# Strassen's seven-block product for the first matmul of the second feed-forward layer, operands in one arena

## The chip, the core and the metric

The kernel runs on one core of a Trainium2 chip. The metric is device time in microseconds (us) of one execution. Engines are named as the profile names them: PE is the matrix engine (PEld its weight loads), DVE the vector engine, ACT the scalar engine, POOL the GpSimd engine, SP the engine that issues the DMAs. "Columns" are the elements per partition that an instruction streams: a matmul of 384 columns has a 128 x 384 moving operand against a 128 x 128 stationary one.

## What is computed

Block-local attention over chunks of 64 makes x (2304 tokens x 512). Two feed-forward layers follow:

```python
def _moe_ref(x, w_in, w_out):                  # layer 1, 2048 features
    h = np.maximum(x @ w_in, 0.0)
    return (h * h @ w_out).astype(np.float32)

def _moe2_ref(x, domain_probs, w1, w2):        # layer 2, E = 4 experts of F = 1024 features
    p = domain_probs / (domain_probs.sum(-1, keepdims=True) + 1e-09)
    out = np.zeros((N, D), dtype=np.float32)
    for e in range(E):
        h = np.maximum(x @ w1[e], 0.0)
        out += p[:, e:e + 1] * (h @ w2[e])
    return out
```

The sizes are N = 2304 tokens, D = 512, E = 4, F = 1024. All inputs of layer 2 are float32. The change concerns `x @ w1[e]`.

## The kernel before

**Split operands.** Every float32 operand of a product is kept as two halves in the type float32r, hi (a rounded copy, written by ACT) and lo (what the copy leaves out, by a subtraction). Each product is three matmuls: hi by hi, hi by lo, lo by hi.

**Steps.** Both layers run in passes of G = 4 feature tiles of 128. Layer 1 has 4 passes, layer 2 has 8 (two for each expert). A pass goes over five token blocks of 384, 384, 512, 512 and 512 tokens (`BLOCKS`), and over the 4 feature tiles in each: 20 steps a pass, 80 steps for layer 1 and 160 for layer 2. A step of `l1` (matmul line L286) multiplies 4 slices of the inner dimension by 3 products, 12 matmuls as wide as the block, into one PSUM bank. ACT and DVE make the hidden tile's halves `gh` and `gl` from it (in layer 2 lines L305 and L307; in layer 1 there is a square between, L297 to L301). A step later `l2` (L332) multiplies them into accumulators. In layer 1 these are 4 x 3 matmuls as wide as the block. In layer 2 the hidden tile is the stationary operand and the weights move, so each 128 tokens take 3 matmuls of 512 columns: 9 a step in a block of 384, 12 in one of 512.

**Evacuation.** After 4 feature tiles the accumulators leave PSUM: in layer 1 by L365 and L367, in layer 2 by L378 (first pass) and L380 (the others: multiply by the expert's probability and add). The last pass's tiles go out by DMA (L385).

**Between the layers.** `split_x` (L347 on ACT, L348 on DVE) makes the halves of layer 1's result while layer 1 still runs.

**Weights.** SP loads a unit of 256 KB (L107), ACT copies it (L145), POOL subtracts (L146). In layer 2 each weight is loaded once. Four units of hidden weights and four of output weights are held in each of two rings.

**Order.** `tc.manual_schedule()` keeps the instructions in the order of the text on each engine, and each engine works its queue in that order. The framework adds the waits that the operands need. PSUM has eight banks: one with the tag "h", four "a", three "t".

Of the kernel before, what the change touches and what calls it, by code (L numbers as in the profile page):

```python
# [42 lines left out]
def tile_kernel(ctx, tc, q, k, v, moe_w_in, moe_w_out, moe2_p, moe2_w1, moe2_w2, out):  # L43
# [13 lines left out]
    npass = npass1 + E * nf2 // G  # L57
# [3 lines left out]

    const = ctx.enter_context(tc.tile_pool(name="const", bufs=1))
    xp = ctx.enter_context(tc.tile_pool(name="xp", bufs=1))
    wpa = ctx.enter_context(tc.tile_pool(name="wpa", bufs=RING_A))
    rawp = ctx.enter_context(tc.tile_pool(name="rawp", bufs=RAW_BUFS))
    cvp = ctx.enter_context(tc.tile_pool(name="cvp", bufs=CV_BUFS))
    gp = ctx.enter_context(tc.tile_pool(name="gp", bufs=LAG + 1))
    rp = ctx.enter_context(tc.tile_pool(name="rp", bufs=1))
    ps = ctx.enter_context(tc.tile_pool(name="ps", bufs=1, space=bass.MemoryType.PSUM))
    att = ExitStack()  # L70
    qkp = att.enter_context(tc.tile_pool(name="qkp", bufs=2))
    late = {}

# [10 lines left out]
    raw, cv, halves = {}, {}, {}  # L84

    def unit_load(n, which):
        if n < nf1:
            r = rawp.tile([P, DM, 2], I32, tag="raw", name="raw")
            if which == 0:
                nc.sync.dma_start(  # L90
                    out=r.rearrange("p (k f) w -> p k (f w)", k=KD),
                    in_=moe_w_in[:, 2 * n * P:2 * (n + 1) * P].rearrange("(k p) f -> p k f", p=P),
                )
            else:
                nc.sync.dma_start(
                    out=r.rearrange("p f w -> p (f w)"), in_=moe_w_out[n * P:(n + 1) * P, :]
                )
        else:
            e, f = divmod(n - nf1, nf2)
            r = rawp.tile([P, DM], F32, tag="raw", name="raw")  # L100
            if which == 0:
                nc.sync.dma_start(
                    out=r.rearrange("p (k f) -> p k f", k=KD),
                    in_=moe2_w1[e, :, f * P:(f + 1) * P].rearrange("(k p) f -> p k f", p=P),
                )
            else:
                nc.sync.dma_start(out=r, in_=moe2_w2[e, f * P:(f + 1) * P, :])  # L107
        raw[n, which] = r

    def unit_convert(n, which):  # L110
        """float64 (two 32-bit words) to the nearest float32; beyond float32's range it
        saturates, below its normal range it becomes zero."""
        r = raw.pop((n, which))
        if n >= nf1:
            cv[n, which] = r
            yield
            return
# [22 lines left out]
    def unit_split(n, which):  # L140
        a = cv.pop((n, which))
        pool = wpa if n % (RING_A + RING_B) < RING_A else late["w"]
        h = pool.tile([P, DM], F32R, tag=f"h{which}", name=f"h{which}")
        l = pool.tile([P, DM], F32R, tag=f"l{which}", name=f"l{which}")
# [7 lines left out]
    # Heads j and j+4 (x = 0, 1) share a tile of 128 partitions.  # L152
# [8 lines left out]
    def new_x(tb):  # L161
        xh[tb] = xp.tile([P, KD, BLOCKS[tb]], F32R, tag=f"xh{tb}", name=f"xh{tb}")
        xl[tb] = xp.tile([P, KD, BLOCKS[tb]], F32R, tag=f"xl{tb}", name=f"xl{tb}")
# [111 lines left out]
    steps = [(p, tb, f) for p in range(npass) for tb in range(NB) for f in range(G)]  # L275
# [3 lines left out]
    def l1(i):  # L279
# [12 lines left out]
        hi = gp.tile([P, 512], F32R, tag="gh", name="gh")  # L292
        lo = gp.tile([P, 512], F32R, tag="gl", name="gl")
        gh[i], gl[i] = hi, lo
        if p < npass1:
            r = rp.tile([P, 512], F32, tag="r", name="r")
            nc.scalar.activation(out=r[:, :T], in_=ph[:, :T], func=AF.Relu)  # L297
            nc.vector.tensor_tensor(out=r[:, :T], in0=r[:, :T], in1=r[:, :T], op=ALU.mult)  # L298
            yield
            nc.scalar.copy(hi[:, :T], r[:, :T])  # L300
            nc.vector.tensor_tensor(  # L301
                out=lo[:, :T], in0=r[:, :T], in1=hi[:, :T].bitcast(F32), op=ALU.subtract
            )
        else:
            nc.scalar.activation(out=hi[:, :T], in_=ph[:, :T], func=AF.Relu)  # L305
            yield
            nc.vector.scalar_tensor_tensor(  # L307
                out=lo[:, :T],
                in0=ph[:, :T],
                scalar=0.0,  # L310
                in1=hi[:, :T].bitcast(F32),
                op0=ALU.max,
                op1=ALU.subtract,
            )

    def l2(i):
# [4 lines left out]
        for d in range(KD if p < npass1 else T // P):  # L321
# [3 lines left out]
            if p < npass1:  # L325
                o = pacc[d][:, :T]
                prods = ((bh[:, ds], hi[:, :T]), (bh[:, ds], lo[:, :T]), (bl[:, ds], hi[:, :T]))
            else:
                o = pacc[d]
                prods = ((hi[:, ds], bh), (hi[:, ds], bl), (lo[:, ds], bh))  # L330
# [8 lines left out]
    later = []  # L339

    def split_x(n):
        for _ in range(min(n, len(later))):
            tb, d = later.pop(0)
            if d == 0:
                new_x(tb)
            a = acc[tb][:, d, :]
            nc.scalar.copy(xh[tb][:, d, :], a)  # L347
            nc.vector.tensor_tensor(  # L348
                out=xl[tb][:, d, :], in0=a, in1=xh[tb][:, d, :].bitcast(F32), op=ALU.subtract
            )  # L350

    def new_acc(tb, shape):
        pool = xp if tb < ACC_EARLY else late["x"]
        acc[tb] = pool.tile(shape, F32, tag=f"acc{tb}", name=f"acc{tb}")

    def evacuate(p, tb, d):
        T = BLOCKS[tb]
        nt = T // P
        pa = pacc.pop(d)
        if p < npass1:  # L360
            if p == 0 and d == 0:
                new_acc(tb, [P, KD, T])
            a = acc[tb][:, d, :]
            if p == 0:
                nc.scalar.copy(a, pa[:, :T])  # L365
            else:
                nc.vector.tensor_tensor(out=a, in0=pa[:, :T], in1=a, op=ALU.add)  # L367
            if p == npass1 - 1:
                later.append((tb, d))
        else:  # L370
            if p == npass1 and d == 0:
                new_acc(tb, [P, nt, DM])
# [48 lines left out]
    with tc.manual_schedule():  # L421
# [44 lines left out]
        for which in range(2):  # L466
            s0_stage(0, "ttthaaaa", which)
# [70 lines left out]
```

## Time and profile before

| | |
|---|---|
| time, median of 3 runs | 1301.8 us (1301.67 to 1302.4) |
| span of the profiled execution, first to last instruction | 1300.4 us |
| PE busy | 1265.9 us, 97% |
| PEld busy | 1088.6 us, 84% |
| DVE busy | 517.0 us, 40% |
| ACT busy | 329.8 us, 25% |
| POOL busy | 209.9 us, 16% |
| mean granted PE clock | 0.986 |

The span lies 1.4 us under the median. The times of single instructions, and the place of each, are those of the one profiled execution. A matmul's end is modelled, and successive matmuls overlap in the record, so the pace of PE is read from the distance between the starts of matmuls and not from the duration of one. The page cuts the span into 40 slices of 32.5 us: attention and layer 1 fill the first 15 of them or so, layer 2 the rest.

### The profile page before, as it was taken

The page shows a single profiled execution, that of the slowest core. Times are in us where ns is not written, and L with a number is a line of the kernel's source. Part 1 is how long each engine was busy: PE and PEld are TensorE (multiplying, and loading weights), DVE is VectorE, ACT ScalarE, POOL GpSimd, SP SyncE. Part 2 cuts the span into 40 slices and gives each one's busy share as a digit, 9 for nine tenths or more (in the row PEclk, how much of TensorE's full clock was granted, in tenths as well). Part 3 has the DMA queues.
Part 4 walks back from the last instruction along what each step waited for, and adds up shares of the span by engine and source line. Part 5 has one row for each costly group of instructions (what it writes and reads, how often), then busy time and mean ns, then how long its engine had stood idle before and what let it go on. Part 6 is the DMA issues. An engine that isn't in the chain of part 4 may idle for free.

```text
span 1300.4 us, 16632 instructions
## 1 busy us (share of the span) xinstructions
PE 1265.9 (97%) x6952; PEld 1088.6 (84%) x6952; DVE 517.0 (40%) x902; ACT 329.8 (25%) x615; POOL 209.9 (16%) x166
## 2 busy tenths in 40 slices
PE   5799997999999999999999999999999999999998
PEld 4698886989989988888888888888888888888887
DVE  5976768664763554111222222222222222222222
ACT  3555543332332333322111111111111111111110
POOL 2420145431440110100110110110110110110000
PEclk7799998999999999999999999999999999999999
DMA  7846022210100000000000100100100100100011
GB/s 191 181 102 160 18 67 66 61 52 18 49 27 14 25 25 17 25 25 14 28 25 9 33 25 9 33 25 9 33 25 9 33 25 9 33 1 1 34 49 65
DMA packets 94843, 53.55 MB, mean 41 GB/s; under 512 B 61744, under 2 KB 86320, under 8 KB 94768
## 3 DMA queue, kind: packets, MB, share of 16 engines
q1 hardware_dynamic: 94768, 52.48, 14.6%
q8 instruction: 55, 0.90, 0.3%
q14 instruction: 20, 0.16, 0.0%
HBM read 47.75 MB, written 4.72 MB: 40 GB/s over the span
## 4 chain that ended last, share of the span: by engine, by line
PE 92%; DVE 5%; issue 1%; SPq 1%; ACT 1%; DMA 0%
PE psa L332 45%; PE pst L286 31%; PE psh L286 13%; PE pst L257 1%; PE pst L215 1%; PE pst L200 1%; DVE cv L122 1%; DVE cv L123 1%; DVE cv L132 1%; PE pst L242 1%; DVE r L298 0%; DMA raw<-in_moe_w_in 0%; SPq L188 0%; SPq L179 0%; DVE e L222 0%
## 5 line engine op out<-in xcount | busy, mean ns | idle before, releaser
L286 PE MATMUL pst<-xh,l 128*128 128x512 f32 (+1 forms) x672 | 247.8, 369 | 0.0
L286 PE MATMUL pst<-xh,h 128*128 128x512 f32 (+1 forms) x672 | 247.5, 368 | 0.0
L286 PE MATMUL pst<-xl,h 128*128 128x512 f32 (+1 forms) x672 | 247.4, 368 | 0.0
L332 PE MATMUL psa<-h,gl 128*128 128x512 f32 x576 | 225.4, 391 | 0.0
L332 PE MATMUL psa<-l,gh 128*128 128x512 f32 x576 | 225.2, 391 | 0.0
L332 PE MATMUL psa<-h,gh 128*128 128x512 f32 x576 | 224.0, 389 | 0.0
L146 POOL TENSOR_TENSOR l<-raw,h 128x512 fp32r<-128x512 f32 x64 | 82.6, 1291 | 705.2 <-ACT h L145 705.2
L305 ACT ACTIVATE gh<-pst 128x512 fp32r<-128x512 f32 (+1 forms) x120 | 66.7, 556 | 496.6 <-PE pst L286 496.6
L307 DVE SCALAR_TENSOR_TENSOR gl<-pst,gh 128x512 fp32r<-128x512 f32 (+1 forms) x120 | 76.1, 634 | 278.2 <-ACT gh L305 278.2
L380 DVE SCALAR_TENSOR_TENSOR acc<-psa,prob,acc 128x512 f32<-128x512 f32 x126 | 89.1, 744 | 151.9 <-PE psa L332 151.9
L286 PEld LDWEIGHTS pst<-xl,h 128*128 128x128 f32 x672 | 126.1, 188 | 18.2
L286 PEld LDWEIGHTS pst<-xh,h 128*128 128x128 f32 x672 | 126.2, 188 | 18.1
L286 PEld LDWEIGHTS pst<-xh,l 128*128 128x128 f32 x672 | 126.1, 188 | 15.9
L332 PE MATMUL psa<-gh,h 128*128 128x512 f32 (+1 forms) x320 | 121.3, 379 | 6.7 <-ACT gh L300 6.0
L332 PEld LDWEIGHTS psa<-h,gl 128*128 128x128 f32 x576 | 108.1, 188 | 22.7
L332 PEld LDWEIGHTS psa<-l,gh 128*128 128x128 f32 x576 | 108.1, 188 | 21.2
L332 PEld LDWEIGHTS psa<-h,gh 128*128 128x128 f32 x576 | 108.1, 188 | 20.7
L332 PE MATMUL psa<-gl,h 128*128 128x512 f32 (+1 forms) x320 | 118.8, 371 | 0.7 <-DVE gl L301 0.7
L332 PE MATMUL psa<-gh,l 128*128 128x512 f32 (+1 forms) x320 | 118.4, 370 | 0.0
L286 PE MATMUL psh<-xl,h 128*128 128x384 f32 (+1 forms) x288 | 106.7, 370 | 3.4 <-DVE xl L270 3.4
L286 PE MATMUL psh<-xh,h 128*128 128x384 f32 (+1 forms) x288 | 109.0, 378 | 0.0
L286 PE MATMUL psh<-xh,l 128*128 128x384 f32 (+1 forms) x288 | 106.6, 370 | 0.0
(92 smaller groups left out, 1282.3 us busy)
## 6 DMA issues: line engine op xcount, KB each, us to landing
raw<-in_moe_w SPq DMA_DIRECT2D x64, 256.0 KB, 2.8
raw<-in_moe_w_in SPq DMA_DIRECT2D x16, 512.0 KB, 4.0
raw<-in_moe_w_out SPq DMA_DIRECT2D x16, 512.0 KB, 3.7
out<-acc SPq DMA_DIRECT2D x18, 256.0 KB, 2.0
q<-in_q SPq DMA_DIRECT2D x32, 128.0 KB, 3.5
k<-in_k SPq DMA_DIRECT2D x32, 128.0 KB, 3.2
v<-in_v SPq DMA_DIRECT2D x32, 80.0 KB, 3.0
v<-in_v SPq DMA_DIRECT2D x32, 64.0 KB, 2.7
```

The costliest lines, as they stand in the source:

```text
L122: nc.vector.tensor_scalar(out=a, in0=hi, scalar1=0x7FFFFFFF, scalar2=None, op0=ALU.bitwise_and)
L123: nc.vector.tensor_scalar(out=af, in0=af, scalar1=F64_MIN, scalar2=F64_MAX, op0=ALU.max, op1=ALU.min)
L132: nc.vector.scalar_tensor_tensor(out=a, in0=a, scalar=0x7FFFFFFF, in1=hi, op0=ALU.bitwise_and, op1=ALU.bitwise_or)
L146: nc.gpsimd.tensor_tensor(out=l, in0=a, in1=h.bitcast(F32), op=ALU.subtract)
L200: nc.tensor.transpose(out=pt[:, j, :], in_=a[:, j].rearrange("p x d -> p (x d)"), identity=ident)
L215: nc.tensor.matmul(pt[x][cs, j, :], lhsT=qt[r, j, cs], rhs=kt[r, j, cs], start=True, stop=True)
L242: nc.tensor.transpose(out=pt[:, j, :], in_=e[:, j, :], identity=ident)
L286: nc.tensor.matmul(ph[:, :T], lhsT=w[:, kk, :], rhs=x[tb][:, kk, :], start=(kk == 0 and n == 0), stop=(kk == KD - 1 and n == 2),)
L305: nc.scalar.activation(out=hi[:, :T], in_=ph[:, :T], func=AF.Relu)
L307: nc.vector.scalar_tensor_tensor(out=lo[:, :T], in0=ph[:, :T], scalar=0.0, in1=hi[:, :T].bitcast(F32), op0=ALU.max, op1=ALU.subtract,)
L332: nc.tensor.matmul(o, lhsT=w, rhs=y, start=(f == 0 and n == 0), stop=(f == G - 1 and n == 2))
L380: nc.vector.scalar_tensor_tensor(out=a, in0=pa, scalar=pe, in1=a, op0=ALU.mult, op1=ALU.add)
```

## The change

Layer 2 is written anew, and layer 1 keeps its steps.

- The 2304 tokens form three groups of 768, and each group goes through all experts before the next begins. Each step n (48 in all) takes one group and two feature tiles of one expert.
- In a step, `x @ w1` for two halves of 384 tokens, two halves of the inner dimension and two feature tiles is eight block products. Strassen's scheme (in Winograd's form) makes them of seven: `c_unit` runs seven units of 2 x 3 = 6 matmuls of 384 columns, on sums and differences of blocks, into three PSUM accumulators b, c and d. `c_finish` snapshots b three times (`snap`, ACT), adds the snapshots to c and d (DVE) and makes the four hidden tiles (`hidden`: ACT, then DVE).
- `d_unit` makes the output of 128 tokens from the two feature tiles of the step before: 6 matmuls of 512 columns into one bank. `d_finish` evacuates it after those 6 (before, after 12). The units of c and d alternate on PE.
- The sums of x (`y_combine`) and those of the weights (`w1_add`) are made by POOL. Their halves are made by ACT and POOL (weights), and ACT with DVE or POOL (x). Since the three groups go through all weights in turn, each weight is loaded, summed and split three times.
- All float32r operands lie in one SBUF tile, the arena `ar`. Layer 1's x, its first ring of weights and the hidden halves are slices of it too, and layer 2's operands reuse their places.
- `split_x` goes. The preparation of layer 2's first group (`y_combine(0)`, the first `w1_add` and `w1_split`) runs during layer 1's last pass.

The diff, cut to what the text below speaks of:

```diff
+HALF = 384
+NSUP = 3
+SWAP = 63
...
+    XW = 2 * KD * NT
+    AR = XW + RING_A * 4 * DM + (LAG + 1) * 2 * 512
+    ar = arena.tile([P, AR], F32R, name="ar")
+    RING_AT, GP_AT = XW, XW + RING_A * 4 * DM
+    NY, NW, NG = 14 * 2 * HALF, 14 * 2 * P, 8 * HALF
+    Y_AT = 0
+    W1_AT = [NY + NW + 4 * DM + NG, NY]
+    W2_AT = [W1_AT[0] + NW, NY + NW]
+    G_AT = [W2_AT[0] + 4 * DM, NY + NW + 4 * DM]
+    assert G_AT[0] + NG <= AR
...
+            o = RING_AT + (n % RING_A * 4 + 2 * which) * DM
+            h, l = ar[:, o:o + DM], ar[:, o + DM:o + 2 * DM]
+        else:
+            h = late["w"].tile([P, DM], F32R, tag=f"h{which}", name=f"h{which}")
+            l = late["w"].tile([P, DM], F32R, tag=f"l{which}", name=f"l{which}")
...
+        o, w = 2 * KD * starts[tb], KD * BLOCKS[tb]
+        xh[tb] = ar[:, o:o + w].rearrange("p (k t) -> p k t", k=KD)
+        xl[tb] = ar[:, o + w:o + 2 * w].rearrange("p (k t) -> p k t", k=KD)
...
+        o = GP_AT + i % (LAG + 1) * 1024
+        hi, lo = ar[:, o:o + 512], ar[:, o + 512:o + 1024]
...
+    def sub(o, a, b):
+        nc.gpsimd.tensor_tensor(out=o, in0=a, in1=b, op=ALU.subtract)
...
+        if sp == 0:
+            for i in (Y11, Y21, Y22):
+                yield from y_split(sp, i)
+        sub(t1, y12, y11)
+        yield
+        sub(t3, y22, y12)
+        yield
+        sub(t2, y22, t1)
+        yield
+        sub(t4, y21, t2)
...
+    def y_split(sp, i):
+        h, l = y_slot(i)
+        a = comb[sp][i]
+        nc.scalar.copy(h, a)
+        eng = nc.vector if sp == 0 or i % 2 == 0 else nc.gpsimd
+        eng.tensor_tensor(out=l, in0=a, in1=h.bitcast(F32), op=ALU.subtract)
...
+    def w1_add(n, part):
+        r = raw1[n]
+        o, a, b, op = (
+            (4, 0, 3, ALU.add), (5, 4, 1, ALU.subtract), (6, 1, 0, ALU.subtract), (7, 2, 5, ALU.subtract)
+        )[part]
+        nc.gpsimd.tensor_tensor(out=r[:, o], in0=r[:, a], in1=r[:, b], op=op)
...
+    def w1_split(n, part):
+        c = NW // 4
+        if part == 0:
+            o = W1_AT[n % 2]
+            w1c[n] = ar[:, o:o + NW // 2], ar[:, o + NW // 2:o + NW]
+        h, l = (y[:, part * c:(part + 1) * c] for y in w1c[n])
+        a = raw1[n].rearrange("p s k f -> p (s k f)")[:, 2 * P + part * c:2 * P + (part + 1) * c]
+        nc.scalar.copy(h, a)
+        nc.gpsimd.tensor_tensor(out=l, in0=a, in1=h.bitcast(F32), op=ALU.subtract)
...
+    UNITS = ((0, Y11), (1, Y21), (4, T2), (3, T1), (5, T3), (2, T4), (6, Y22))
+    g, st = {}, {}
+    def c_unit(n, u):
+        ws, ys = UNITS[u]
+        if u == 0:
+            st["b"] = bank("t")
+            o = G_AT[n % 2]
+            g[n] = [
+                [ar[:, o + (2 * i + z) * HALF:o + (2 * i + z + 1) * HALF] for z in range(2)] for i in range(4)
+            ]
+        elif u == 1:
+            st["c"] = bank("h")
+        elif u == 3:
+            st["d"] = bank("t")
+        p = st["bcbdbbd"[u]][:, :HALF]
...
+        for kk in range(2):
+            for z, (w, y) in enumerate(((wh, yh), (wh, yl), (wl, yh))):
+                nc.tensor.matmul(
+                    p, lhsT=w[:, kk, :], rhs=y[:, kk, :],
+                    start=(kk == 0 and z == 0 and u in (0, 1, 3)),
+                    stop=(kk == 1 and z == 2 and u in (1, 5, 6)),
+                    skip_group_check=True,
...
+    def snap(nm, p):
+        s = st[nm] = late["s"].tile([P, HALF], F32, tag=nm, name=nm)
+        nc.scalar.copy(s, p)
+    def hidden(n, i, p):
+        h, l = g[n][i]
+        nc.scalar.activation(out=h, in_=p, func=AF.Relu)
+        nc.vector.scalar_tensor_tensor(
+            out=l, in0=p, scalar=0.0, in1=h.bitcast(F32), op0=ALU.max, op1=ALU.subtract
+        )
+    def c_finish(n, u):
+        b, c, d = (st[x][:, :HALF] if x in st else None for x in "bcd")
+        if u == 0:
+            snap("s1", b)
+        elif u == 1:
+            nc.vector.tensor_tensor(out=c, in0=c, in1=st["s1"], op=ALU.add)
+            hidden(n, 0, c)
+        elif u == 2:
+            snap("u2", b)
+        elif u == 4:
+            snap("u3", b)
+            nc.vector.tensor_tensor(out=c, in0=d, in1=st["u3"], op=ALU.add)
+            hidden(n, 3, c)
+        elif u == 5:
+            hidden(n, 2, b)
+        elif u == 6:
+            nc.vector.tensor_tensor(out=d, in0=d, in1=st["u2"], op=ALU.add)
+            hidden(n, 1, d)
...
+    def d_unit(n, t):
+        tau, tt = divmod(t, 3)
+        ts = slice(tt * P, (tt + 1) * P)
+        bh, bl = w2c[n]
+        p = st["o"] = bank("a")
+        for i in range(2):
+            hi, lo = g[n][2 * i + tau]
+            for z, (w, y) in enumerate(((hi, bh), (hi, bl), (lo, bh))):
+                nc.tensor.matmul(
+                    p, lhsT=w[:, ts], rhs=y[:, i, :], start=(i == 0 and z == 0), stop=(i == 1 and z == 2)
...
+        early = {
+            SWAP: [(w1_load, (0,)), (w1_load, (1,)), (w2_load, (0,))],
+            LEAD + NS - 4: [(w1_split, (0, 0)), (w1_split, (0, 1)), (w1_load, (2,))],
+        }
+        for i in range(4):
+            early[SWAP + 5 + i] = [(w1_add, (0, i))]
+            early[LEAD + NS - 8 + i] = [(w1_add, (1, i))]
+        y0_at = LEAD + (npass1 - 1) * G * NB + 2 * G + LAG
...
+        for n in range(NQ + 1):
+            sp, m = divmod(n, E * NP)
+            last = m == E * NP - 1 and sp + 1 < NSUP
+            if m == 2:
+                if sp == 1:
+                    pend["y"] = y_gather()
+                else:
+                    pend["y"] = iter(())
+            if m == 6 and sp + 1 < NSUP:
+                pend["y"] = y_combine(sp + 1)
+            for u in range(7):
+                if n < NQ:
+                    c_unit(n, u)
+                    if n == u == 0:
+                        run(ch)
+                        lw.close()
+                        sn = ctx.enter_context(tc.tile_pool(name="sn", bufs=1, side="right", reuse_waits="tile"))
+                        late["s"] = sn
+                        late["o"] = sn.tile([P, 6, DM], F32, name="o")
+                    c_finish(n, u)
+                    if last:
+                        for _ in y_split(sp + 1, UNITS[u][1]):
+                            pass
+                    elif u == 5 and "y" in pend:
+                        next(pend["y"], None)
+                    if u in (0, 1) and n + 1 < NQ:
+                        w1_split(n + 1, u)
+                    if u == 1 and n + 3 < NQ:
+                        w1_load(n + 3)
+                    if u in (2, 3):
+                        w2_split(n, u - 2)
+                    if u == 3 and n + 1 < NQ:
+                        w2_load(n + 1)
+                    if u >= 3 and n + 2 < NQ:
+                        w1_add(n + 2, u - 3)
+                if n > 0 and u < 6:
+                    d_unit(n - 1, u)
+                    d_finish(n - 1, u)
```

## Rows read from the trace of the kernel before

**Rows 1.** The page, parts 1 and 2: busy time, and the span in 40 slices.

```profile
PE 1265.9 (97%) x6952; PEld 1088.6 (84%) x6952; DVE 517.0 (40%) x902; ACT 329.8 (25%) x615; POOL 209.9 (16%) x166
...
PE   5799997999999999999999999999999999999998
...
PEclk7799998999999999999999999999999999999999
```

**Rows 2.** Layer 2's windows: length; busy PE, PEld, DVE, ACT, POOL; clock, DMA, GB/s.

```profile
503.40:602.20 98.80, 98.80 (x458) 84.43 (x457) 18.52 (x29) 26.65 (x46) 10.31 (x8) 1.00 0.08 22
...
sum 792.90, PE 792.90 PEld 677.28 DVE 189.93 ACT 131.56 POOL 72.21; mean PE 99.11 PEld 84.66 DVE 23.74 ACT 16.45 POOL 9.03
```

**Rows 3.** PE timeline (start, duration): ends of long runs of equal matmuls; layer 2's first.

```profile
347.50 0.39 PE L332 MATMUL psa<-gh,h 128*128 128x512 f32 x1
...
404.62 0.33 PE L286 MATMUL pst<-xh,h 128*128 128x384 f32 x1
...
411.59 0.33 PE L332 MATMUL psa<-gh,h 128*128 128x384 f32 x1
...
438.63 0.39 PE L286 MATMUL pst<-xh,h 128*128 128x512 f32 x1
...
503.38 0.33 PE L286 MATMUL pst<-xh,h 128*128 128x384 f32 x1
```

**Rows 4.** PE timeline in layer 2 where the matmuls change their width, and ACT behind.

```profile
602.15 0.33 PE L286 MATMUL pst<-xh,h 128*128 128x384 f32 x1
...
603.22 0.33 PE L286 MATMUL pst<-xh,h 128*128 128x384 f32 x1
...
604.26 0.39 PE L332 MATMUL psa<-h,gh 128*128 128x512 f32 x1
...
604.45 0.49 ACT L305 ACTIVATE gh<-pst 128x384 fp32r<-128x384 f32 x1 [4.23 <-PE pst L286]
...
605.64 0.39 PE L332 MATMUL psa<-h,gh 128*128 128x512 f32 x1
...
607.02 0.33 PE L286 MATMUL pst<-xh,h 128*128 128x384 f32 x1
```

**Rows 5.** Groups by line and form: operands, count, busy us, mean ns of one, idle before.

```profile
L286 PEld LDWEIGHTS pst<-xl,h 128*128 128x128 f32 x672 | 126.1, 188 | 18.2
...
L305 ACT ACTIVATE gh<-pst 128x384 fp32r<-128x384 f32 x48 | 23.6, 492 | 175.9 <-PE pst L286 175.9
L307 DVE SCALAR_TENSOR_TENSOR gl<-pst,gh 128x384 fp32r<-128x384 f32 x48 | 26.6, 554 | 93.6 <-ACT gh L305 93.6
L347 ACT CAST xh<-acc 128x512 fp32r<-128x512 f32 x12 | 6.8, 617 | 0.0
L347 ACT CAST xh<-acc 128x384 fp32r<-128x384 f32 x8 | 3.7, 509 | 0.0
```

**Rows 6.** Single lines of DVE and POOL: min/median/max ns, first and last start.

```profile
L380 DVE SCALAR_TENSOR_TENSOR acc<-psa,prob,acc x126: 739/742/752, 622.6 to 1296.5; 128x512 f32<-128x512 f32 x126
...
L348 DVE TENSOR_TENSOR xl<-acc,xh x20: 545/683/1369, 430.6 to 517.6; 128x512 fp32r<-128x512 f32 x12, 128x384 fp32r<-128x384 f32 x8
...
L146 POOL TENSOR_TENSOR l<-raw,h x64: 1285/1288/1306, 418.2 to 1177.1; 128x512 fp32r<-128x512 f32 x64
...
L137 POOL TENSOR_TENSOR cv<-cv,raw x32: 1278/1576/1644, 19.7 to 386.9; 128x512 f32<-128x512 f32 x32
```

**Rows 7.** DMA issues: count, KB each, us to landing.

```profile
raw<-in_moe_w SPq DMA_DIRECT2D x64, 256.0 KB, 2.8
```

**Rows 8.** The end of layer 2: last matmul, last evacuations.

```profile
1296.06 0.39 PE L332 MATMUL psa<-h,gl 128*128 128x512 f32 x1
...
1295.80 1.43 DVE L380 SCALAR_TENSOR_TENSOR acc<-psa,prob,acc 128x512 f32<-128x512 f32 x2
```

**Rows 9.** Timeline in the attention stage: ACT and DVE on one `raw` tile.

```profile
29.09 0.69 ACT L121 ACTIVATE raw<-raw 128x512 f32<-128x512 uint32 x1
29.38 0.42 DVE L122 TENSOR_SCALAR cv<-raw 128x512 int32<-128x512 int32 x1
```

More of the change, by code (lines that the diff above doesn't have):

```diff
@@ L56, in tile_kernel @@
     npass1 = nf1 // G
-    npass = npass1 + E * nf2 // G
     NB = len(BLOCKS)
@@ L272, in s3_stage @@
             )
-    steps = [(p, tb, f) for p in range(npass) for tb in range(NB) for f in range(G)]
+    steps = [(p, tb, f) for p in range(npass1) for tb in range(NB) for f in range(G)]
     NS = len(steps)
@@ L337, in l2 @@
             yield
[L339 to L354, printed above, removed]
@@ new lines, in evacuate @@
+        a = acc[tb][:, d, :]
+        if p == 0:
+            nc.scalar.copy(a, pa[:, :T])
+        else:
+            nc.vector.tensor_tensor(out=a, in0=pa[:, :T], in1=a, op=ALU.add)
+    NP = nf2 // 2
+    NQ = NSUP * E * NP
+    rows = {}
+    for sp in range(NSUP):
+        if sp < NSUP - 1:
+            r = [starts[2 * sp] + i * P for i in range(3)] + [starts[2 * sp + 1] + i * P for i in range(3)]
+        else:
+            r = [starts[NB - 1] + i * P for i in range(3)] + [starts[2 + i] + HALF for i in range(3)]
+        rows[sp] = r
@@ new lines, in y_split, with y_gather @@
+    def y_split(sp, i):
[4 more added lines that the diff above has]
+        eng.tensor_tensor(out=l, in0=a, in1=h.bitcast(F32), op=ALU.subtract)
+        yield
+    def y_gather():
+        for i in range(3):
+            nc.gpsimd.tensor_scalar(
+                out=acc[0][:, :, i * P:(i + 1) * P], in0=acc[2 + i][:, :, HALF:], scalar1=1.0,
+                scalar2=None, op0=ALU.mult,
+            )
+            yield
@@ new lines, in tile_kernel, with w1_load @@
+    raw1, raw2, w1c, w2c = {}, {}, {}, {}
+    def w1_load(n):
+        e, j = divmod(n % (E * NP), NP)
+        r = raw1[n] = late["raw"].tile([P, 8, 2, P], F32, tag="raw1", name="raw1", bufs=2)
+        for i, h0, h1, slot in ((0, 0, 2, 1), (1, 0, 1, 0), (1, 1, 2, 3)):
+            f0 = (2 * j + i) * P
+            nc.sync.dma_start(
+                out=r[:, slot:slot + h1 - h0].rearrange("p h k f -> p (h k) f"),
+                in_=moe2_w1[e, h0 * 2 * P:h1 * 2 * P, f0:f0 + P].rearrange("(k p) f -> p k f", p=P),
+            )
@@ new lines, in w2_load @@
+    def w2_load(n):
+        e, j = divmod(n % (E * NP), NP)
+        r = raw2[n] = late["raw"].tile([P, 2, DM], F32, tag="raw2", name="raw2", bufs=1)
+        nc.sync.dma_start(
+            out=r, in_=moe2_w2[e, 2 * j * P:2 * (j + 1) * P, :].rearrange("(h p) d -> p h d", p=P)
+        )
+    def w1_add(n, part):
[4 more added lines that the diff above has]
+        nc.gpsimd.tensor_tensor(out=r[:, o], in0=r[:, a], in1=r[:, b], op=op)
@@ L501, in tile_kernel @@
             else:
-                run(ch, KD + 2)
-                conv = do(r, "convert")
-                for c in conv:
-                    next(c)
-                run(ch, 1)
-                for c in conv:
-                    run(c)
-                do(r, "split")
-                if m % G != LAG - 1:
-                    split_x(2)
-            run(ch)
+                if r == SWAP:
+                    staging.close()
+                    late["raw"] = ctx.enter_context(tc.tile_pool(name="raw", bufs=1, reuse_waits="tile"))
@@ new lines, in tile_kernel @@
+                for fn, args in early.pop(r, ()):
+                    fn(*args)
+                if r > y0_at:
+                    next(late.setdefault("y0", y_combine(0)), None)
+                if m < NS:
+                    run(ch, KD + 2)
+                    conv = do(r, "convert")
+                    for c in conv:
+                        next(c)
+                    run(ch, 1)
+                    for c in conv:
+                        run(c)
+                    do(r, "split")
+            if m < NS:
+                run(ch)
```

182 lines of the change are left out of this document (90 added, 92 removed).

## The prediction

> **What bounds the kernel now.** I read the page's busy time and slices first. PE is busy 97% of the span, and at its full granted clock (9 in every slice from the twelfth on), while DVE is at 40%, ACT at 25% and POOL at 16% [rows 1]. A mean says little of one stage, so I went on to layer 2 pass by pass. From its first matmul at 503.38 [rows 3] to the end of the last one's slot (1296.06 + 0.23, [rows 8]) are 792.9 us. [...] The first 2.76 us of `l2` there belong to layer 1's last step (12 matmuls, as long as the run from 604.26 to 607.02, [rows 4]); layer 2 itself takes 790.1.
>
> So the question is what a matmul costs by its width. Two long runs tell it, by the distance between their ends: 252 matmuls of 512 columns from 347.50 to 404.62, 226.7 ns each, and 156 of 384 from 411.59 to 438.63, 173.3 ns each [rows 3]. [...]
>
> [...] The first six matmuls of 384 after a run of 512 take 1.07 us (602.15 to 603.22), six at the steady pace 1.04; the first six of 512 after 384 take 1.38 (604.26 to 605.64), against 1.36 [rows 4]. Over a pass: 96 matmuls of 384 and 360 of 512 at the steady prices are 98.24 us, and the pass from 503.38 to 602.15 took 98.77 [rows 3, 4]. It has 8 runs of each width, so one pair of changes costs 0.066 us when the runs are long, and 0.05 within the first six.
>
> **The change part by part.**
>
> *Fewer columns.* Each of the 48 steps has 7 x 6 = 42 matmuls of 384 columns and 6 x 6 = 36 of 512. That makes 2016 x 173.3 ns = 349.4 us and 1728 x 226.7 ns = 391.7 us, 741.1 in all, against 790.1. The second product keeps its 1728 matmuls; the gain is an eighth of the first product's columns (110,592, 46 us), less 96 matmuls more (1.3 us), plus the 4.2 us that changes of width cost now. [...]
>
> *More changes of width.* The units of 384 and of 512 alternate: six pairs of changes a step, 288 in all. No row shows runs as short as six. The ends are 0 (a short run leaves the pipe as it was) and twice the six-matmul cost, 0.11 us; I take 0.056, between the 0.05 of the first six and the 0.066 of a whole run, which is the nearest row. That is 16.1 us, between 0 and 32.
>
> *The accumulator chain.* PE now waits inside a step for ACT: unit 5 adds to b, which `snap` must have read after unit 4. ACT begins 0.20 us after the last matmul's slot (604.45 against 604.26, [rows 4]) and takes 0.49 [rows 5], and between units 4 and 5 stand six matmuls of 512, 1.36 us. About 0.6 us are left over. The other snapshots (after units 0 and 2) have a whole further unit of 1.04 besides, and d is read by DVE 3.5 us before unit 6 writes it. So it costs nothing while ACT is on time. In step 0 there is no output to alternate with: there unit 4 waits for the snapshot after unit 2, which ACT reaches only after `hidden` and half of `w1_split` (0.8 us by the same durations), and unit 5 for the one after unit 4 (0.75). That makes 1.6 us, between 0 and 4.
>
> *Loads of the other engines in a step* (PE's share: 741.1 + 16.1 over 48, 15.8 us). DVE: 6 evacuations of 742 ns [rows 6] and 7 instructions on 384 columns at 554 [rows 5], 8.3 us. It evacuates twice as often as before. ACT: 7 instructions of 0.49, two copies of 896 columns (from 509 ns for 384 and 617 for 512, [rows 5], 0.94 each) and two of 512, 6.6 us. POOL: subtractions over 2 x 896 and 2 x 512 columns and four sums over 256, 3840 columns at 1288 ns for 512 [rows 6], 9.7 us; at the dearest two-operand line there, 1644 ns, 12.3. `y_combine` adds 1.9 us in each of four steps before a group ends, and `y_gather` less in three. All of it fits under 15.8. SP: 1 MB a step, in transfers like those that land in 2.8 us [rows 7], and issued more than a step ahead; `w1_load` waits for POOL's split and has `w2_load` queued behind it, which has 5 us or more to spare. The weights come three times, at 66 GB/s.
>
> *The ends of groups.* In the last step of the first two groups the splits of x come on top: four by DVE, three by POOL (1.9 each). DVE then has 12.4 us and POOL 15.5. The splits on DVE have both inputs in SBUF, and such a line shows 545 to 1369 ns, median 683, next to evacuations from PSUM that never leave 739 to 752 [rows 6]: something holds the former up by up to 0.69 us, and POOL was at work then. [...] Four banks for the output units take up a few us of delay. I take 2 us for both ends together, between 0 and 12 (DVE 5.7 us over its step, twice).
>
> *The end of layer 1.* `split_x` goes, and nothing of PE with it. In its place POOL makes sums and splits during the last pass, while layer 1's square and subtraction, both with two SBUF inputs on DVE, stand between `l1` and `l2`. That chain has 5.4 us (24 matmuls of 512) for some 3. Held up twice by a subtraction of 2.3 us it would be late: 1 us, between 0 and 4.
>
> *The tail* (last matmul, one evacuation, DMA) stays as it is [rows 8]. Attention and layer 1's first three passes stay; the arena moves their operands, and nothing in their order.
>
> The sum: 741.1 + 16.1 + 1.6 + 2 + 1 = 761.8 us for 790.1, 28.3 less. From the median of 1301.8 (span 1300.4 and 1.4 around it) that makes 1273.5 us.
>
> **The rivals.**
>
> *Snapshots late (slower).* If ACT reaches the snapshot after unit 4 later than 0.6 us past its time, each step loses the rest, and the whole gain (28.3 / 48 = 0.59 us a step) is gone when ACT is 1.2 us late. For it: ACT works in order, and its `hidden` instructions wait for DVE's additions, which stand behind evacuations of 0.74. One half of `w1_split` and one `hidden` in the way, with the wait between them (1.9 us), would lose 1.3 us a step: 1273.5 + 62 = 1335 us. Against it: the long copies are queued after units 0 to 3, and by the durations above ACT has been idle for two to three us when unit 4 ends.
>
> *Changes of width dearer than twice the row.* If a short run pays the 0.066 of a whole pair several times over, the gain shrinks by 288 times the excess: 0.15 us a pair makes 27 us more than I take, 1300 us, no change. For it: nothing like it is in the trace. Against it: the extra cost within a run is spent after six to ten matmuls.
>
> *The arena watched as one tile (the change doesn't do what it says).* If the framework orders accesses to `ar` by the tile and not by the slice, each unit on PE waits for the splits queued before it: by the durations above 3.2 us after unit 0, 4.8 after unit 1, 1.9 twice, then 2.1, 1.0 and 1.6, some 16.5 us a step, 790 in all, so 2060 us. Against it: DVE reads one interleaved half of a `raw` tile (29.38) while ACT still writes the other (29.09 to 29.78, [rows 9]), so slices are told apart there.
>
> *POOL the bound.* It decides from 4.1 ns a column (15.8 us for 3840); at twice the price of today's split the step takes 19.4 us and the kernel 1446. The dearest line seen makes 3.2.
>
> **How the numbers follow.** A measurement of this kernel can tell about 0.2%, 2.6 us, from no change. My forecast (PE bound, 1253 to 1291) has 0.83. Dearer changes of width have 0.07, of which half stays over 0.2% faster and half ends within it; late snapshots 0.06, of which 0.01 falls within 0.2%; the arena 0.03; POOL 0.01. So faster 0.865, same 0.045, slower 0.09. The low end is the sum with no cost at all for changes, step 0 and ends (741.1: 49 us off, 1253). The high end is the changes at their dearest with the others as taken (1289.4), and a little of the others' bounds: 1291. All at their dearest at once would be 1305, which I leave out.
>
> **What would show it.** Right: in steady steps, starts of matmuls 173 and 227 ns apart with a little more after each change, no idle time of PE, and a step of about 15.8 us; POOL near 65% busy; a gap of one or two us in step 0. A pace of 173 and 227 from the first matmul of each unit puts the time near 1257; one well over 180 and 235 throughout, near 1290. Wrong: a gap in front of unit 5 or 6 in every step, with ACT's copy as what released it; PE waiting for POOL at unit 0; or layer 1 longer than its 503 us.

## The result

The changed kernel takes 1266.6 us (1265.0 to 1266.9), the one before 1301.9: a ratio of 0.972, 95% interval 0.9706 to 0.9733, 35.3 us less where 28.3 less were forecast. The time lies inside the range; the terms that were off are taken up below.

The page after it, busy time and slices, answers to [rows 1]:

```profile
PE 1229.4 (97%) x7048; PEld 1088.8 (86%) x7048; DVE 725.0 (57%) x1217; ACT 505.9 (40%) x920; POOL 630.8 (50%) x507
...
PE   5799997999999999999999999999999999999998
...
POOL 2420036431343022666776686767766866666650
PEclk7799999999999999999999999999999999999999
```

PE has 36.5 us less to do and is as full as before. POOL's work has tripled; over all of layer 2 it is 64% busy (484.0 of 754.9 us), where near 65% was forecast. The windows show a steady step, the last step of the first group, the step after it, and the whole of layer 2, in the columns of [rows 2] (length; busy PE, PEld, DVE, ACT and POOL; clock, DMA share, GB/s):

```profile
533.40:549.00 15.60, 15.60 (x80) 14.02 (x79) 8.25 (x13) 6.11 (x11) 9.58 (x8) 1.00 0.25 69
736.70:752.30 15.60, 15.60 (x80) 14.02 (x79) 11.31 (x15) 10.39 (x17) 11.73 (x7) 1.00 0.12 35
752.30:768.00 15.70, 15.70 (x80) 14.12 (x79) 10.96 (x16) 6.64 (x12) 14.96 (x13) 1.00 0.42 127
...
506.20:1261.10 754.90, 753.95 (x3757) 676.75 (x3755) 397.72 (x619) 312.87 (x559) 484.04 (x391) 1.00 0.23 70
```

In the steady step DVE, ACT and POOL carry about what the loads of a step promised (8.3, 6.6 and 9.7 us), and PE is busy for all of each of the three steps, at the end of the group too. The list of PE's waits after 500 us has one row (us in total, times, longest), the two waits of step 0:

```profile
PE pst L493 <- ACT u L502: 0.9, 2, 0.6
```

The chain of work (start, us, what) shows a step, from one run of 12 matmuls of 384 (unit 6 and the next step's unit 0) to the next:

```profile
532.54 2.08 PE pst L493 x12
534.62 1.39 PE psa L538 x6
536.01 1.04 PE psh L493 x6
...
548.18 1.91 PE pst L493 x11
```

A step is 15.64 us (548.18 less 532.54). Six matmuls of 512 take 1.39, 0.03 more than at the steady pace of [rows 3]; six of 384 take 1.04, as at that pace. Layer 2's first and last matmuls in PE's timeline, to be set against 503.38 [rows 3] and 1296.06 [rows 8]:

```profile
506.18 1.22 PE L493 MATMUL pst<-ar 128*128 128x384 f32 x6
...
1259.25 1.98 PE L538 MATMUL psa<-ar 128*128 128x512 f32 x8
```

The last of those eight matmuls starts 0.39 before the row's end, at 1260.84, so layer 2 lasts 754.9 us, or 752.1 without layer 1's last 2.8. It was 790.1: 38.0 us are gained there. Layer 1 gives 2.8 of them back, for layer 2 begins at 506.18.

### The profile page after: what moved, and what is told of

Same layout as the page of the kernel before. It is cut to its first block, busy times and chain, and to the rows that moved or that the text cites. A ratio compares the mean times of both kernels' runs of the same rounds, so it can differ in the third digit from the quotient of the medians.

```text
span 1265.1 us, 18239 instructions
## 1 busy us (share of the span) xinstructions
PE 1229.4 (97%) x7048; PEld 1088.8 (86%) x7048; DVE 725.0 (57%) x1217; ACT 505.9 (40%) x920; POOL 630.8 (50%) x507
## 4 chain that ended last, share of the span: by engine, by line
PE 92%; DVE 4%; SPq 2%; issue 1%; ACT 1%; DMA 1%; DVEq 0%
PE psa L538 32%; PE pst L493 24%; PE psa L323 15%; PE pst L293 9%; PE psh L293 6%; PE psh L493 4%; PE pst L264 1%; SPq L186 1%; PE pst L222 1%; SPq L195 1%; PE pst L207 1%; DVE cv L125 1%; DVE cv L126 1%; DVE r L304 0%; PE pst L249 0%
## 5 line engine op out<-in xcount | busy, mean ns | idle before, releaser
L538 PE MATMUL psa<-ar 128*128 128x512 f32 x1728 | 445.7, 393 | 0.0
L538 PEld LDWEIGHTS psa<-ar 128*128 128x128 f32 x1728 | 320.0, 188 | 50.3
L461 POOL TENSOR_TENSOR ar<-raw,ar 128x896 fp32r<-128x896 f32 x96 | 204.1, 2128 | 274.4 <-ACT ar L460 274.4
L493 PE MATMUL pst<-ar 128*128 128x384 f32 x1728 | 339.2, 335 | 0.9 <-ACT u L502 0.9
L493 PEld LDWEIGHTS pst<-ar 128*128 128x128 f32 x1728 | 307.3, 188 | 22.9 <-ACT u L502 1.6
L551 DVE SCALAR_TENSOR_TENSOR o<-psa,prob,o 128x512 f32<-128x512 f32 x270 | 201.5, 747 | 173.3 <-PE psa L538 173.3
L451 POOL TENSOR_TENSOR raw<-raw 128x256 f32<-128x256 f32 x192 | 141.2, 754 | 8.6 <-DMA raw<-in_moe_w 5.0
L470 POOL TENSOR_TENSOR ar<-raw,ar 128x512 fp32r<-128x512 f32 x96 | 123.4, 1305 | 12.5 <-ACT ar L469 12.5
L323 PE MATMUL psa<-ar 128*128 128x512 f32 (+1 forms) x480 | 112.5, 374 | 0.0
L323 PE MATMUL psa<-ar,h 128*128 128x512 f32 (+1 forms) x320 | 95.0, 378 | 7.5 <-ACT ar L306 6.2
L323 PEld LDWEIGHTS psa<-ar 128*128 128x128 f32 x480 | 86.3, 188 | 12.2 <-DVE ar L307 0.3
```

Of the source, the lines that this page charges most:

```text
L323: nc.tensor.matmul(o, lhsT=w, rhs=y, start=(f == 0 and n == 0), stop=(f == G - 1 and n == 2))
L451: nc.gpsimd.tensor_tensor(out=r[:, o], in0=r[:, a], in1=r[:, b], op=op)
L493: nc.tensor.matmul(p, lhsT=w[:, kk, :], rhs=y[:, kk, :], start=(kk == 0 and z == 0 and u in (0, 1, 3)), stop=(kk == 1 and z == 2 and u in ...
L538: nc.tensor.matmul(p, lhsT=w[:, ts], rhs=y[:, i, :], start=(i == 0 and z == 0), stop=(i == 1 and z == 2))
L551: nc.vector.scalar_tensor_tensor(out=o, in0=p, scalar=pe, in1=o, op0=ALU.mult, op1=ALU.add)
```

## The experiments

**Eight products for seven.** The layout, the groups and the alternation stay; the sums and snapshots go.

```diff
-    UNITS = ((0, Y11), (1, Y21), (4, T2), (3, T1), (5, T3), (2, T4), (6, Y22))
+    UNITS = ((1, Y11), (2, Y21), (0, Y11), (3, Y21), (1, T1), (2, Y22), (0, T1), (3, Y22))
...
-        sub(t1, y12, y11)
+        c[T1] = y12
...
-            snap("s1", b)
...
+        if u % 2 == 1:
+            hidden(n, (0, 2, 1, 3)[u // 2], st["c"][:, :HALF])
```

> The changed kernel with eight block products for seven: the sums of x and of the weights and the snapshots are gone, each hidden tile is the plain sum of two products, and the layout, the three groups, the short output units and their alternation stay. Theory (the seventh part less columns is the gain, and all else costs): a step has 48 matmuls of 384 for 42, so it takes 15.64 + 6 x 0.1733 = 16.68 us; with the 1.5 us of waits in step 0 gone the kernel takes 1266.6 + 49.9 - 1.5 = 1315 us, 13 slower than before. Rival (the new layout and the shorter accumulation bring the gain, and the sums cost what the seventh product saves): no slower than 1270 us.

It took 1314.1 us, 1.0083 of the kernel before (1.0065 to 1.0100). Its chain has steps of 16.67 to 16.69 us (16.67 is 580.29 less 563.62):

```profile
563.62 3.12 PE pst L483 x18
...
580.29 3.12 PE pst L483 x18
```

So one product less is worth 47 us, close to what its columns say (48 x 1.04, less the 1.5 of step 0, is 48.4), and the sums and splits that it needs cost PE nothing outside step 0. The rest of the change costs some 11 us: the same columns as before in 384 more matmuls (5.1 us at the 13.3 ns that the prices of [rows 3], 226.67 and 173.33 ns, leave beside their slope of 0.4167 ns a column), more changes of width (5.3), and 1.0 in layer 1, taken up below.

**Output units in pairs.** Three pairs of changes of width a step for six, by the order alone.

```diff
-                if n > 0 and u < 6:
-                    d_unit(n - 1, u)
-                    d_finish(n - 1, u)
+                for t in {1: (0, 1), 3: (2, 3), 4: (4, 5)}.get(u, ()) if n > 0 else ():
+                    d_unit(n - 1, t)
+                    d_finish(n - 1, t)
```

> The changed kernel with its output units in pairs behind units 1, 3 and 4, so three pairs of changes of width in a step for six. Theory (the extra cost is a transient that grows with the length of the run behind a change: 29 ns in the first six matmuls of 512 and 41 in all of a long run; 4 ns for 384 after a short run, 26 after a long one): 3 x 0.067 = 0.20 us a step as now, a step of 15.64 us, 1266.6 us within 1. Rival (each change has its price, 0.033 us a pair): 0.10 us a step less, a step of 15.54, 1261.8 us.

It took 1265.2 us (ratio 0.9708, 0.9693 to 0.9723). The step is the same 15.64 us, with half the changes:

```profile
561.40 3.14 PE pst L493 x18
565.58 2.76 PE psa L538 x12
568.35 2.10 PE pst L493 x12
...
577.04 3.14 PE pst L493 x18
```

Here twelve matmuls of 384 take 2.10 us, and 18 take 3.14, both 0.02 above the steady pace; in the changed kernel twelve take 2.08, at the pace. So in these two kernels what a change costs hangs on how long the runs before and after it are: 0.20 us a step for six pairs of changes, and 0.20 for three.

**Output units as narrow as the others.** All of layer 2's matmuls have 384 columns. The kernel leaves out the last 128 columns of the output, and its evacuations are narrower too.

```diff
-                    p, lhsT=w[:, ts], rhs=y[:, i, :], start=(i == 0 and z == 0), stop=(i == 1 and z == 2)
+                    p[:, :HALF], lhsT=w[:, ts], rhs=y[:, i, :HALF], start=(i == 0 and z == 0), stop=(i == 1 and z == 2)
```

> The output units compute 384 of their 512 columns (the last 128 columns of the output stay zero), so all matmuls of layer 2 have one width, and units, banks and waits stay. Theory (the extra cost comes from the change of width): every matmul takes 173.3 ns, a step 78 x 0.1733 = 13.52 us, the kernel 1266.6 - 48 x 2.12 = 1165 us. Rival (it comes with each new unit: another bank, other weights, a wait that is long satisfied): a step of 13.52 + 0.20 = 13.72 us, 1174 us.

It took 1166.8 us (one execution), and the chain has steps of 13.52 us, 78 matmuls of 173.3 ns and nothing besides:

```profile
557.44 2.08 PE pst L493 x12
559.52 1.04 PE psa L538 x6
...
570.96 2.08 PE pst L493 x12
```

The 0.20 us come from the change of width; new banks, new weights and satisfied waits cost nothing.

**The third snapshot late.** Two more copies of b ahead of it.

```diff
+            snap("v1", b)
+            snap("v2", b)
             snap("u3", b)
```

> Two more copies by ACT of accumulator b (into tiles that nothing reads) ahead of the third snapshot, behind unit 4. Theory (the snapshot has 0.6 us to spare under the output unit of 1.39 us): 0.20 + 3 x 0.49 = 1.67 us, 0.3 us more than the output unit, so PE waits about 0.3 us in front of unit 5 in each step and the kernel takes some 16 us more, 1278 to 1290. Rival (the snapshot is well hidden, or unit 5 does not wait for it): 1266.6 within 2. If there is nothing to spare already: 0.98 us a step, 1314 us.

It took 1281.1 us (one execution), 14.4 more than the changed kernel. The timeline shows the stretch (output unit, the copies, the weight loads and matmuls of unit 5), the waits of PEld after 500 us their sum, and the chain the step of 15.93 us:

```profile
561.09 1.55 PE L540 MATMUL psa<-ar 128*128 128x512 f32 x6
561.34 0.86 ACT L502 COPY v<-pst 128x384 f32<-128x384 f32 x2 [3.35 <-PE pst L493]
562.09 0.50 ACT L502 COPY u<-pst 128x384 f32<-128x384 f32 x1
562.64 0.99 PEld L493 LDWEIGHTS pst<-ar 128*128 128x128 f32 x6 [0.43 <-ACT u L502]
562.64 1.32 PE L493 MATMUL pst<-ar 128*128 128x384 f32 x6
...
PEld pst L493 <- ACT u L502: 22.7, 49, 1.7
...
565.36 2.08 PE pst L493 x12
...
581.29 2.08 PE pst L493 x12
```

The copies end at 562.59 and unit 5 starts at 562.64, so it does wait for them. PE's own rows don't show so short a wait, because the modelled end of the matmul before lies over it; PEld's do, 49 times here, and in the changed kernel only the two times of step 0. Three copies back to back take 1.25 us where one takes 0.48, and 0.77 us more cost 0.29 (15.93 for 15.64): the snapshot has about 0.5 us to spare, for the 0.6 forecast. The rival of the late snapshots was a real mechanism with its place and price; ACT is on time.

**More work for POOL.** Each subtraction of the split hidden weights twice, then three times.

```diff
-        nc.gpsimd.tensor_tensor(out=l, in0=a, in1=h.bitcast(F32), op=ALU.subtract)
+        for _ in range(2 if n > 1 else 1):
+            nc.gpsimd.tensor_tensor(out=l, in0=a, in1=h.bitcast(F32), op=ALU.subtract)
```

> POOL makes each subtraction of the split hidden weights twice, so its work in a step goes from 9.9 to 14.1 us under a step of 15.64. Theory (POOL is off the path and decides only from a load of 15.6 us a step): 1266 to 1271 us, the few us at the two ends of groups, where the splits of x bring POOL to some 20 us in one step. Rival (POOL's results are needed sooner than its mean load tells): some us in every step, over 1290 us.

> The same subtraction three times: 18.4 us of POOL in a step. Theory: POOL is now the bound, a step takes 18.4 us (some 2 more where x is combined), 46 x 2.75 + 30 = 157 us more, 1400 to 1430 us. Rival (PE still sets the pace, POOL's record is rough): under 1300 us.

Twice took 1272.1 us, a little above the 1266 to 1271 expected; three times took 1423.4 (one execution each). The rows are PE's waits of the one, then those of the other and a window of it:

```profile
PE psa L539 <- POOL ar L471: 4.3, 4, 1.9
```

```profile
PE psa L539 <- POOL ar L471: 94.7, 84, 3.6
...
600.00:800.00 200.00, 177.59 (x805) 153.30 (x803) 91.02 (x140) 69.22 (x121) 195.93 (x129) 0.93 0.18 53
```

With 14 us of POOL in a step the steady step stays at 15.64 us, and nothing moves but the four waits behind the two ends of groups; with 18 POOL is busy 98% and sets the time. The point of decision lies where it was forecast, between these two.

**Layer 1's second ring moved by 192 bytes.** In the second and fourth pass of layer 1 the matmuls of 512 had become dearer, 2.75 us for twelve against 2.72. These are the passes whose weights come from the second ring. By the addresses in the compiled program, which no trace shows, that ring lies 480 bytes past a multiple of 512 in the changed kernel, and x 288 past; before, both were 288 past.

```diff
+                pad = lw.enter_context(tc.tile_pool(name="pad", bufs=1, side="right"))
+                pad.tile([P, 48], F32, name="pad")
                 late["w"] = lw.enter_context(tc.tile_pool(name="wpb", bufs=RING_B, side="right"))
```

> The second ring of layer 1's weights is moved by 192 bytes, so that its tiles start at the same place within 512 bytes as before the change. Theory (the 2.2 ns by which the 512-column matmuls of layer 1's second and fourth pass became dearer hang on where that ring lies): these passes are back at 226.7 ns a matmul, layer 2 begins 1.1 to 1.2 us earlier, 1265.4 us. Rival (it is something else, POOL's or the DMAs' traffic): no difference, 228.9 ns as now.

It took 1264.1 us (0.9702, 0.9683 to 0.9721). Two more runs put the arena 0 bytes past a multiple of 512 with the ring, and 480 past like the ring where it was:

> The changed kernel with the arena moved by 224 bytes and layer 1's second ring by 480, so that all operands of the matmuls start at a multiple of 512 bytes (before: 288 bytes past one, the ring 480 past one in the changed kernel). Theory A (what counts is that stationary and moving operand lie alike): 173.3 and 226.7 ns a matmul as now, layer 1's second and fourth pass back at 226.7, 1264 to 1266 us. Theory B (what counts is the place itself: the dearer ring's 480 cost 2.2 ns more than 288, and 0 may cost less): another pace in all of layer 2, by the same 2.2 ns 3744 + 1920 matmuls would take 12 us less, some 1253 us, or more if the place is a bad one.

> The changed kernel with the arena moved by 192 bytes, so that its operands start 480 bytes past a multiple of 512, as layer 1's second ring does in the changed kernel; the ring stays. Theory A (stationary and moving operand have to lie alike): 226.7 ns a matmul of 512 columns in layer 1's second and fourth pass, steps of 15.64 us, 1263 to 1266 us. Theory B (480 bytes past is a bad place for the stationary operand): 228.9 ns in these passes as now, and 2.2 ns more for each of the 3744 matmuls of layer 2, steps of 15.81 us, 1274 us.

They took 1263.4 us (0.9697, 0.9684 to 0.9710) and 1264.1 (0.9705, 0.9688 to 0.9723), with steps of 15.64. The chain in layer 1's last pass, one row each of the changed kernel, the moved ring, the arena at 0 and the arena at 480:

```profile
495.35 2.75 PE pst L293 x12
```

```profile
494.69 2.72 PE psa L323 x12
```

```profile
495.02 2.72 PE psa L324 x12
```

```profile
470.92 2.72 PE pst L294 x12
```

At each of the three places, 2.72 comes back when stationary and moving operand lie alike, so theory A holds and B falls. Two things stay open: only one unlike pair was measured (480 and 288), and 512 bytes need not be the unit, for 192 bytes apart is unlike within 128 or 256 too. The chains tell the theories apart and the times don't, for they scatter by more (layer 2 begins at 502.69, 503.01 and 503.40 in these three traces). The ring's place is worth 1.0 us: in the chain, layer 2 begins 263.5 us behind the second pass's first run of 512 in the changed kernel, and 262.5 behind it before and with the ring moved. The 2.2 ns for each of 576 matmuls make 1.3 of that, and some 0.3 comes back, as beside the dearer matmuls the changes of width show no extra cost (2.75 and 2.08 for twelve, elsewhere 2.76 and 2.10).

**One run of output units.** Units in the order 0, 3, 2, all output units, 4, 1, 5, 6.

```diff
-            for u in range(7):
+            for u in (0, 3, 2):
                 if n < NQ:
                     c_unit(n, u)
...
+            for t in range(6):
+                if n > 0:
+                    d_unit(n - 1, t)
+                    d_finish(n - 1, t)
...
+            for u in (4, 1, 5, 6):
+                if n < NQ:
+                    c_unit(n, u)
```

> All six output units in one run (36 matmuls of 512) between units 2 and 4, units in the order 0, 3, 2, output, 4, 1, 5, 6, with unit 1 covering the third snapshot, the sum of d and u3 in a bank of its own, and the finish of unit 6 behind the next step's first snapshot: one pair of changes of width a step. Theory (transient by length of run): 15.44 + 0.067 = 15.51 us a step, 0.13 less, 1260.2 us, if no unit waits. Rival (each change has its price of 0.033 us a pair): 15.47 us, 1258.6 us. If the chain isn't covered any more, a wait in each step: 0.3 us would bring 1275.

It took 1265.3 us (0.9710, 0.9694 to 0.9727), no better than the order it replaces, though the chain's steps are the 15.51 us expected (580.25 less 564.74):

```profile
564.74 8.20 PE psa L551 x36
572.94 1.06 PE pst L493 x6
...
580.25 8.20 PE psa L551 x36
```

The 6 us that the steps gain (47 x 0.13) went at the two ends of groups, where one step each is 4.0 us longer. First PE's waits, then windows of the first of them (columns as above):

```profile
PE psh L493 <- POOL ar L414: 4.3, 2, 2.1
...
760.00:762.40 2.40, 0.26 (x2) 0.00 (x0) 1.26 (x3) 0.97 (x2) 2.40 (x3) 1.00 0.25 66
762.40:766.00 3.60, 3.60 (x12) 3.60 (x13) 1.58 (x3) 0.49 (x1) 2.74 (x4) 0.53 0.93 332
```

POOL's split of one block of x came 2.3 us late, and behind the wait the granted clock stood at 0.53 for 3.6 us, which cost the rest, 1.7 (0.47 x 3.6). The second version queues that split ahead of the output weights' splits, and moves the ring.

```diff
-                    if t < 2:
-                        w2_split(n, t)
...
                     if t < len(late_y):
                         for _ in y_split(sp, late_y[t]):
                             pass
...
+                    if t in (2, 3):
+                        w2_split(n, t - 2)
```

> The kernel with one run of output units, with the splits of x at a group's end queued on POOL ahead of the output weights' splits, and layer 1's second ring moved by 192 bytes. Theory (the 4.0 us lost at each of two group ends are POOL's split of one block of x, queued too late, and what the halved granted clock of some 3 us behind that wait adds): 15.51 us in every step from the second on, 8.0 us less than the 1265.3 of the first version of this order, and 0.9 for layer 1: 1256.4 us within 2, for the start of the kernel differs by that much between runs. Rival (DVE's and POOL's splits hold each other up whatever their order): a loss of 2 us or more at each group's end stays, 1260 to 1264.

It took 1257.4 us, 0.9657 of the kernel before (0.9644 to 0.9670), the best version here: some 45 us less than before, and 8 to 9 less than the change. Of the 9 between the medians, 6 are the steps; 3.2 lie ahead of layer 2 (its first matmul at 503.00 for 506.18), where the moved ring accounts for 1.0 and the rest is the scatter of the kernel's start taken up below. Its waits from 500 us on, and its chain across the first group's end:

```profile
PE pst L493 <- ACT u L502: 0.6, 1, 0.6
...
749.84 8.20 PE psa L551 x36
...
765.36 8.20 PE psa L551 x36
```

## Why the prediction was right, and where it was off

*The bound, right.* PE sets the time before (busy for all of layer 2, at clock 1.00, [rows 2]) and after (753.95 of 754.90 us, at 1.00), and the gain is an eighth of the first product's columns. Eight products in the same layout give all of it back and more.

*Fewer columns, right.* 741.1 us at the two steady prices, plus 9.5 for changes of width (0.20 in each of the 47 steps that have output units, and 0.05 in the last run of output units) and 1.5 for step 0, are the 752.1 measured.

*Changes of width, too dear.* 16.1 us were taken, 9.5 measured. The mechanism was right (narrow output units leave none of it: 13.52 us are 78 matmuls of 173.3 ns), the size was off: 0.056 us a pair against 0.033. I read the price of a run of 384 behind a *long* run of 512 (1.07 us for six, [rows 4]), and behind a run of six it is 1.04: none at all. The 512 side costs 0.03 (1.39 against 1.36), where I had read 0.02. The paired order, where the 384 side costs 0.02 again, shows that the length of the run before it decides. This term made 6.6 of the 7 us by which the forecast was too high; that the next two, 2 too high and 1.8 too low, nearly cancel is luck.

*Step 0, right.* Two waits in front of units 4 and 5, forecast 1.6 us, measured 1.5, of which 0.95 are the idle times in the rows below, 0.25 the slower matmuls behind each wait (six in 1.33 us and eight in 1.68, where six elsewhere in the timeline take 1.21 and eight 1.55), and 0.3 the modelled ends of the matmuls ahead of the waits. In the timeline of the changed kernel:

```profile
513.67 1.33 PE L493 MATMUL pst<-ar 128*128 128x384 f32 x6 [0.38 <-ACT u L502]
515.57 1.68 PE L493 MATMUL pst<-ar 128*128 128x384 f32 x8 [0.57 <-ACT u L502]
```

*The ends of groups, 2 us taken, none measured.* The steps there are 15.64 us like the others. The contention itself is there. DVE's splits of x (min/median/max ns), one of POOL's groups (count, busy us, mean ns), and the timeline of POOL and DVE in the first group's last step:

```profile
L414 DVE TENSOR_TENSOR ar<-acc,ar x15: 944/961/2811, 451.4 to 1005.9; 128x768 fp32r<-128x768 f32 x15
...
L470 POOL TENSOR_TENSOR ar<-raw,ar 128x512 fp32r<-128x512 f32 x96 | 123.4, 1305 | 12.5 <-ACT ar L469 12.5
...
744.52 2.12 POOL L461 TENSOR_TENSOR ar<-raw,ar 128x896 fp32r<-128x896 f32 x1
746.61 2.02 POOL L470 TENSOR_TENSOR ar<-raw,ar 128x512 fp32r<-128x512 f32 x1
...
744.66 2.80 DVE L414 TENSOR_TENSOR ar<-acc,ar 128x768 fp32r<-128x768 f32 x1 [1.51 <-ACT ar L412]
```

One split took 2.81 us where the median is 0.96, and its like at the other end of a group 2.80. The latter starts 0.14 us behind a POOL subtraction of 2.12 us and ends 0.82 behind that one's end, which fits a wait for all that was left of it, 1.98 us; POOL's next subtraction then took 2.02 us for a mean of 1.31. The 1.85 us more lie far over the 0.69 that I took as the most from the row before. That row was no bound: in the trace of the kernel before, POOL's subtraction had begun 0.48 us ahead of the two splits, 0.82 us of it were left, and the two took 1.97 us, 0.60 more than two at the median of 0.683.

```profile
476.23 1.30 POOL L146 TENSOR_TENSOR l<-raw,h 128x512 fp32r<-128x512 f32 x1 [9.57 <-ACT h L145]
...
476.71 1.97 DVE L348 TENSOR_TENSOR xl<-acc,xh 128x512 fp32r<-128x512 f32 x2 [0.35 <-ACT xh L347]
```

The four splits on DVE take 0.96, 2.80, 1.50 and 1.51 us at the first end and as much at the second, 5.9 us over the median for both, near the 5.5 that eight times the row's 0.69 make. No run shows the 2 us taken, nor their bound of 12 with DVE 5.7 us over its step at each end: these were my estimates, and in their place the runs show those 5.9 us on DVE and none on PE, with DVE busy for 11.31 of 15.60 us in the first group's last step. The order hid the delay. That four banks of output, and the step between split and use, have the room is argued and not shown; the room is small, for with 4.2 us more of POOL in a step the four waits of 4.3 us stand just there.

*The end of layer 1, near in size by luck.* 1 us was taken for POOL holding up DVE for whole subtractions, and no run shows the term. DVE's square and its subtraction in layer 1's last pass took up to 1.53 and 1.58 us for a median of 0.69 (before, at most 0.69), but PE has no wait from 400 to 506 us. Instead the second ring's place cost 1.0. The prediction names a layer 1 longer than its 503 us as a sign of being wrong, and the sign came: layer 2 begins 2.8 us later. The other 1.8 arose before the second pass's first run of 512, which starts at 242.82 for 241.01 before, and they are a scatter between executions and not a price of the change: with the same instructions up to there, that run starts at 240.33 in the trace with the ring moved and at 241.03 in the one with eight products. What sets it in an execution is open.

*From columns to the gain.* An eighth of the first product's columns (110,592) is 46.1 us at 0.4167 ns each; measured are 38.0. Of the 8.1 between, 1.3 is the 96 matmuls more at 13.3 ns, 5.3 the changes of width (9.5 for 4.2 before) and 1.5 step 0.

*The rivals.* Late snapshots and POOL as the bound are mechanisms with the prices given, and both have room: 0.5 us for the one, between 14 and 18 us of POOL a step for the other. Slices of the arena are told apart, or the steps would not be 15.64. A pair of changes of width costs 0.033 us, less than the row and not more. Where the arena lies makes no difference to layer 2's steps (15.64 us at all three places).

## What to carry to other kernels

Where one engine is busy without a gap, as PE is here for 753.95 of layer 2's 754.90 us, a change is worth its instructions times the pace of that engine, read from long runs of equal ones; what the other engines take on is free up to a load that can be worked out per step (here 14 us of POOL under a step of 15.64, but not 18), and one run with that load raised shows how far. A transient at a change has to be priced for the run lengths that the new order will have (0.033 us a pair here, 0.066 in the longer runs before), and a longer run of each kind can be worth more than a finer alternation (15.51 us a step for 15.64), if the chain behind it is reordered to keep its cover. One late operand on an engine off the path cost more than its wait, 4.0 us for 2.3, where the granted clock stood at 0.53 behind it, so the rare steps (first, last, ends of groups) deserve the same sums as the steady ones.

## What was not expected of the hardware

- In layer 1's last pass matmuls of 512 columns took 226.7 ns (2.72 us for twelve) when stationary and moving operand started alike (both 0, 288 or 480 bytes past a multiple of 512: arena at 0, kernel before and moved ring, arena at 480), and 228.9 (2.75) in the changed kernel, where one lay 480 past and the other 288. Other differences were not tried.
- In the changed kernel a run of six matmuls of 384 between runs of six of 512 cost nothing for the change (1.04 us); behind a run of 12 or more of 512 it was 0.02 us (2.10 for twelve with units in pairs, 1.06 for six with one run of output units) to 0.03 (1.07 for six in the kernel before). A run of 512 behind one of 384 cost 0.03 in its first six matmuls (1.39) and 0.04 in twelve (2.76 with units in pairs).
- In the first version of one run of output units the granted clock was 0.53 for 3.6 us behind a wait of PE of 2.1 us. In the run with POOL three times, with 84 waits of up to 3.6 us, its mean was 0.93 from 600 to 800 us. Behind a wait of 1.9 us in the run with POOL twice five matmuls of 384 took 1.03 us (from 756.25), as five do without a wait in the changed kernel (from 512.26); and behind the waits of 0.4 and 0.6 us in step 0 of the changed kernel the clock was 1.00 (513.60 to 522.00).
- In the changed kernel a DVE subtraction with both inputs in SBUF that started 0.14 us behind a POOL subtraction of 2.12 us took 2.80 us for a median of 0.96, and the POOL subtraction behind it 2.02 for a mean of 1.31.
